# Output stores at slots of their own on a second queue, a spread issued behind the next copy, and one reciprocal per query denominator, with a retimed plan

## The chip, the core and the metric

The kernel runs on one core of one Trainium2 chip. The core has five engines that run at the same time, each with its own in-order instruction queue: TensorE (PE, matrix products into PSUM), VectorE (DVE), ScalarE (ACT), GpSimd (POOL), and SyncE (SP), which here only issues DMA transfers. A DMA can be issued from SP's queue or from ACT's; an instruction that waits holds everything behind it on its own queue. The metric is the device time of one execution in microseconds (us), smaller is better.

## The reference

```python
B, S, D, H = 1, 2048, 640, 32          # Dh = 20; F = 1536
xn = layernorm(x)
q, k, v = heads(xn @ wqkv)
pq, pk = q @ w_phi, k @ w_phi                          # per head, 20x20
phi_q = concat([softmax(pq), softmax(-pq)])            # 40 features per head
phi_k = concat([softmax(pk), softmax(-pk)])
kv = einsum("bhsf,bhsd->bhfd", phi_k, v)
z  = einsum("bhsf->bhf", phi_k)
num = einsum("bhqf,bhfd->bhqd", phi_q, kv)
den = einsum("bhqf,bhf->bhq", phi_q, z)[..., None] + 1e-6
s = merge_heads(num / den) @ wo                        # attention branch
g = silu(gelu(xn @ w1 + b1) @ w2 + b2)                 # gate branch
out = x + s * g
```

All arrays are 32-bit floats. Products that need full accuracy are made of three passes over high and low parts of both operands (high x high, high x low, low x high).

## The kernel before, in words

There are two halves. The first (to about 238 us) normalises x, makes keys, values and queries, and sums `kv` and `z`. It is not touched by the change. The second half runs PE through a **feed-forward** of 12 units and then a **tail**.

*A unit* takes two of the twelve 128-wide tiles of F for one half of the tokens (units 0 to 5 the first half, 6 to 11 the second). Its up projection (line 1275) is seven groups of products from sums of inputs and weights, with the sums undone on DVE (lines 1630 to 1652); ACT applies gelu (`act`) and makes the high part of the hidden layer, DVE the low part (`act_lo`, line 1286). Its down projection (`down`, line 1317) is ten groups of six matmuls, two times five output groups, each added into `y` by DVE (line 1326).

*Alongside*, DVE, ACT, POOL and SP do the rest of the attention for 16 token tiles `t`: load the exponentials (`q_load`), multiply by `z` on POOL (`q_ez`), sum per head (`q_rc`, `q_dn`), combine the sums into one factor per head and sign (`q_den`), scale (`q_scale`, on POOL or DVE), transpose (`q_turn`) and store the features (`q_put2`). They also load and split the weights of later units (`w2_load`, `w2_split`, `w1_step`), rebuild sums of x (`x_load` to `x_store`) and load them (`reload`).

*The tail* has four chunks `c` of 512 tokens. For each, `num_step` multiplies the features by `kv`: step 5 first (eight leftover heads), then 0 to 4. In each of these ACT copies the high part (line 1450) and DVE makes the low part (line 1451). `spread(j)` is a DMA from ACT's queue that puts the leftover rows into tile `j`. `finish(c, d)` then makes output group `d` (128 of the 640 columns): 15 matmuls (line 1514), times the gate on DVE (line 1516), plus x on POOL (line 1517), and a store. Gates of chunks 0 and 1 come from `y` through a silu on ACT (`gate`); those of chunks 2 and 3 were stored earlier and are loaded by `load_res` (line 1492), which also loads the x tile (line 1487).

*The order of the work* is written out by hand. PE's program has 372 + 40 slots: 31 in each unit, two in each output group of the tail. `tick()` emits what `PLAN` has put at the present slot, in order of the fraction; `when(s, f)` puts a call there. So a slot number says behind which other instructions an operation stands on its own engine's queue, and no more: an engine with nothing to wait for runs ahead. `PLAN["c_q"]`, `"c_w2"`, `"c_w1"` and `"c_x"` choose POOL or DVE for single operations. Tiles come from pools with a fixed number of buffers (`slabs` 23, `rows` 11, `phs` and `gts` for leftover features and gates in the tail); a new tile waits for the last user of its buffer. PSUM has eight banks, one for each product group.

In the tail a store of output group (c, d) is put two slots behind the group, on SP's queue:

```python
when(at_slot[0] + 2, nc.sync.dma_start, out_t[d * P:(d + 1) * P, c * CW:(c + 1) * CW], xr[:])
```

Because it is emitted through `tick`, the profile gives it line 1303. The stores of the last two groups are issued directly, in two halves each (line 1519).

Of the kernel before, what the change touches and what calls it, by code (L numbers as in the profile page):

```python
# [15 lines left out]
P = 128  # L16
# [24 lines left out]
def _ft(t):  # L41
# [2 lines left out]

PLAN = {
# [17 lines left out]
    ],  # L63
    "w2": [
        [-36.8, -32.04, 4.35, 3.86],
        [-0.55, 1.21, 31.1, 32.11],
        [28.2, 22.21, 57.6, 53.86],
        [64.2, 66.21, 95.6, 93.61],
        [93.95, 90.46, 124.6, 125.36],
        [120.45, 122.96, 154.85, 156.86],  # L70
        [156.45, 155.46, 183.85, 185.11],
        [192.95, 189.71, 219.6, 219.61],
        [219.95, 222.21, 249.1, 251.61],
        [250.7, 243.96, 278.1, 280.11],
        [279.95, 280.46, 312.85, 312.36],
        [302.2, 305.21, 343.1, 341.11],
    ],
    "w1": [
        [],
        [0.15, 7, 10.6, 15.5, 17, 17.5],  # L80
        [36.15, 43.75, 51.1, 46.75, 47.75, 48.25],
        [62.65, 73, 77.85, 76.5, 77.0, 77.0],
        [92.65, 101.5, 107.1, 107.5, 108.5, 110.0],
        [119.9, 131.75, 138.85, 132.25, 133.25, 134.75],
        [155.9, 165.75, 168.85, 170.75, 172.75, 172.75],
        [187.15, 196.5, 203.1, 203.75, 205.0, 205.75],
        [232.5],
        [264.5],
        [281.25],
        [308.4, 318.0, 323.6, 323.0, 324.0, 324.75],  # L90
    ],
    "keep": [63.0, 90.5, 127.25],
    "x": [
        [26.75, 45.5, 52.3, 66.25, 73.8],
        [63.25, 84.25, 92.8, 107.75, 114.3],
    ],
    "reload": [157.35, 164.11, 160.37, 161.63, 165.89, 162.9, 164.41, 171.17],
    "silu": [191.5, 187.5, 201.75, 195.6, 197.95],
    "wo": [344.15, 334.16, 342.92, 333.43, 336.69, 356.75, 358.5, 361.5, 360.75, 361.75],
    "phi": [  # L100
        [340.85, 341.11, 338.87, 338.13, 337.39, 337.9],
        [359.75, 358.26, 352.52, 355.53, 356.79, 357.05],
        [371.5, 375.75, 372.75, 375.0, 376.0, 377.25],
        [387.25, 387.5, 387.0, 387.75, 390.25, 387.25],
    ],
    "num": [362.01, 377.01, 382.01, 396.01],
    "res": [361.25, 363.1, 374, 373.25, 376, 378.5, 381.5, 380.5, 387.25, 385, 386.5, 388, 395.25, 392.5, 393, 397.75, 395.5, 402.75, 401.0, 406.75],
    "gate": [371.9, 370.91, 375.15, 376.4, 378.9, 378.9, 378.9, 382.4, 385.65, 386.9, 392.65, 392.9, 393.9, 398.9, 396.15, 402.4, 406.9, 403.4, 408.9, 403.9],
    "c_x": ["pool", "pool", "pool", "pool"],
    "c_q": ["pool", "pool", "pool", "pool", "pool", "vector", "pool", "pool", "pool", "pool", "pool", "pool", "pool", "pool", "pool", "vector"],  # L110
    "c_w2": ["pool", "pool", "pool", "pool", "pool", "pool", "vector", "pool", "pool", "pool", "pool", "pool", "pool", "vector", "vector", "pool", "vector", "vector", "vector", "pool", "pool", "pool", "pool", "pool"],
    "c_w1": ["vector", "pool", "pool", "pool", "pool", "vector", "pool", "pool", "vector", "pool", "pool", "pool", "pool", "vector", "pool", "pool", "vector", "pool", "vector", "pool", "pool", "pool", "pool", "pool", "pool", "pool", "pool", "pool", "pool", "pool", "pool", "vector", "pool", "pool", "pool", "pool", "vector", "pool", "pool", "vector", "vector", "vector", "pool", "pool", "vector", "pool", "pool", "pool"],
    "c_wo": ["pool", "pool", "pool", "pool", "pool"],
    "c_oT": ["late", "slab", "late", "slab"],
}

# [2 lines left out]
def hedgehog_gated_mlp_kernel(ctx: ExitStack, tc: tile.TileContext, x, xt_in, wqk, bd, wv, wo, w1, b1, w2, b2, out_t):  # L119
# [1257 lines left out]
        qe[t].append(zv)  # L1377

    def q_rc(t):
        rc = head_sums(qe[t][0], "rc")  # L1380
        nc.vector.reciprocal(rc[:], rc[:])
# [4 lines left out]

    def q_den(t):
        rc, dn = qe[t][2:]
        nc.vector.tensor_tensor(dn[:], dn[:], rc[:], op=OP.mult)
        d3 = dn[:].rearrange("p (h s) -> p h s", s=2)  # L1390
        den = small.tile([P, 32], F32, tag="den", name="den")
        nc.vector.scalar_tensor_tensor(den[:], d3[:, :, 0], DEN_EPS, d3[:, :, 1], op0=OP.add, op1=OP.add)
# [110 lines left out]
    def finish(c, d, oT, last):  # L1503
# [109 lines left out]
    for unit in range(units):  # L1613
# [128 lines left out]
```

## Time and profile before

| what | value |
|---|---|
| runs | 654.72, 652.51, 651.80 us; median 652.51 |
| profiled execution | 652.12 us, its span 650.4 us |
| busy share of the span | PE 98%, PE weight loads 85%, DVE 73%, POOL 59%, ACT 46% |
| granted PE clock over the span | 0.997 |
| DMA | 130.58 MB, mean 201 GB/s |
| feed-forward, up to PE's first numerators of the tail | 238.20 to 545.2 us |
| tail | 545.2 to 650.4 us |

A group row reads: line, engine, operation, output tile <- input tiles, shapes, count | total us, mean ns of one | idle time of the engine just before, and what ended it. A row of the time table begins with its start and its duration in us; in brackets stands how long the engine sat idle before it, and what released it. A row of waits reads: engine, line, what was waited for: us in all, times, the longest. A row of windows has the stretch, its length, the busy time of PE, PE weight loads, DVE, ACT and POOL, then granted clock, DMA share and GB/s.

### The profile page before, as it was taken

How to read it: one execution, taken by the hardware profiler on the slowest of the kernel's cores; microseconds unless marked ns; L12 is line 12 of the kernel's file. 1: busy time of each engine (PE TensorE's matmuls, PEld its weight loads, DVE VectorE, ACT ScalarE, POOL GpSimd, SP SyncE). 2: the span in 40 equal slices, each digit the busy share in tenths (PEclk: the TensorE clock that was granted, in tenths of full speed). 3: DMA queues.
4: the chain of work that ended last, by engine and by line, in shares of the span. 5: the costliest groups of instructions: out<-in, count | busy, mean ns of one | idle time of the engine just before them, and what ended most of it. 6: DMA issues, size and time to landing. Idle time of an engine off the chain costs nothing.

```text
span 650.4 us, 11475 instructions
## 1 busy us (share of the span) xinstructions
PE 639.2 (98%) x4360; PEld 554.0 (85%) x4360; DVE 477.0 (73%) x737; ACT 301.1 (46%) x486; POOL 383.8 (59%) x333
## 2 busy tenths in 40 slices
PE   8999999999999999999999999999999999999797
PEld 8999999999999998888888888888888885758486
DVE  5879987766795666796778668987899897853232
ACT  4556777654566768435243255651231434342110
POOL 3597887775784446979875666335073866332332
PEclk9999999999999999999999999999999999999999
DMA  8436921130932882819939496695646699766955
GB/s 319 191 119 207 283 72 66 42 103 2 310 112 109 304 296 80 282 50 318 341 99 314 175 404 261 193 308 136 241 115 257 197 245 248 217 170 187 303 179 175
DMA packets 119938, 130.58 MB, mean 201 GB/s; under 512 B 46892, under 2 KB 86316, under 8 KB 118988
## 3 DMA queue, kind: packets, MB, share of 16 engines
q1 hardware_dynamic: 119564, 129.21, 61.7%
q10 hardware_dynamic: 320, 0.66, 0.5%
q8 instruction: 34, 0.56, 0.3%
q14 instruction: 20, 0.16, 0.1%
HBM read 81.66 MB, written 46.20 MB: 197 GB/s over the span
## 4 chain that ended last, share of the span: by engine, by line
PE 91%; DMA 3%; POOL 2%; issue 1%; DVE 1%; SPq 1%; ACT 0%; POOLq 0%; DVEq 0%
PE pB L1317 25%; PE pB L1275 22%; PE pW L558 21%; PE pB L1514 9%; PE pA L417 4%; PE pW L1051 3%; PE pB L1446 2%; DMA gt<-g_dram 2%; PE pA L236 2%; PE kv L650 1%; DMA folds<-in_wqk_dram 1%; POOL tt L349 1%; POOL xd L368 0%; PE pA L403 0%; PE pB L1249 0%
## 5 line engine op out<-in xcount | busy, mean ns | idle before, releaser
L1317 PE MATMUL pB<-hs,w2s 128*128 128x512 f32 x720 | 166.3, 390 | 0.8 <-DVE hs L1286 0.8
L1317 PEld LDWEIGHTS pB<-hs,w2s 128*128 128x128 f32 x720 | 134.9, 188 | 30.0 <-DVE hs L1286 1.2
L1275 PE MATMUL pB<-xp,w1s 128*128 128x512 f32 x324 | 81.3, 389 | 0.0
L475 POOL TENSOR_TENSOR eq<-eq,rc 128x1280 f32<-128x1280 f32 x14 | 33.4, 2389 | 79.2 <-DVE rc L1395 69.3
L1275 PE MATMUL pB<-xd,w1s 128*128 128x512 f32 x324 | 79.3, 389 | 0.0
L1326 DVE TENSOR_TENSOR y<-pB,y 128x512 f32<-128x512 f32 x100 | 64.4, 674 | 9.9 <-PE pB L1317 9.9
L1275 PEld LDWEIGHTS pB<-xd,w1s 128*128 128x128 f32 x324 | 60.8, 188 | 12.6
L1275 PEld LDWEIGHTS pB<-xp,w1s 128*128 128x128 f32 x324 | 60.8, 188 | 12.6
L1514 PE MATMUL pB<-oT,wo 128*128 128x512 f32 (+1 forms) x315 | 70.0, 382 | 0.1
L1514 PEld LDWEIGHTS pB<-oT,wo 128*128 128x128 f32 x315 | 57.3, 189 | 14.9 <-issue 3.0
L1280 ACT ACTIVATE pB<-pB,b1t 128x512 f32<-128x512 f32 x48 | 31.8, 662 | 69.7 <-DVE pB L1640 28.8
L456 POOL TENSOR_TENSOR e<-e,mxs 128x1280 f32<-128x1280 f32 x13 | 30.7, 2372 | 41.0 <-DVE mxs L451 29.5
L462 ACT ACTIVATE e<-e 128x1280 f32<-128x1280 f32 x32 | 40.8, 1274 | 17.5 <-POOL e L456 7.9
L558 PE MATMUL pW<-wsum,xd 128*128 128x320 f32 x288 | 48.4, 310 | 0.0
L1376 POOL TENSOR_TENSOR ez<-eq,zrep 128x1280 f32<-128x1280 f32 x16 | 47.4, 2967 | 1.5 <-PE pB L1317 1.5
L1291 ACT ACTIVATE x<-pB 128x512 f32<-128x512 f32 x12 | 7.2, 599 | 78.8 <-PE pB L1275 78.8
L558 PEld LDWEIGHTS pW<-wsum,xd 128*128 128x128 f32 x288 | 43.6, 188 | 0.0
L475 POOL TENSOR_TENSOR e<-e,rc 128x1280 f32<-128x1280 f32 x15 | 36.1, 2409 | 5.8 <-DVE rc L912 4.5
L1517 POOL TENSOR_TENSOR xres<-y,xres 128x256 f32<-128x256 f32 x20 | 14.1, 737 | 38.0 <-issue 22.3
L1286 DVE TENSOR_TENSOR hs<-pB,hs 128x512 fp32r<-128x512 f32 x48 | 31.8, 683 | 3.8 <-ACT hs L1282 3.8
L211 POOL TENSOR_TENSOR w2s<-raw,w2s 128x640 fp32r<-128x640 f32 x18 | 28.7, 1609 | 10.0 <-ACT w2s L209 10.0
L674 POOL TENSOR_TENSOR w1s<-raw,w1s 128x384 fp32r<-128x384 f32 (+1 forms) x14 | 19.0, 1360 | 23.1 <-ACT w1s L673 23.1
(218 smaller groups left out, 1272.8 us busy)
## 6 DMA issues: line engine op xcount, KB each, us to landing
raw<-in_w_dram SPq DMA_DIRECT2D x42, 320.0 KB
e_dram<-e SPq DMA_DIRECT2D x16, 640.0 KB
eq<-e_dram SPq DMA_DIRECT2D x16, 640.0 KB
phi_dram<-pt SPq DMA_DIRECT2D x64, 160.0 KB
ph<-phi_dram SPq DMA_DIRECT2D x20, 480.0 KB
xt<-in_x_dram SPq DMA_DIRECT2D x16, 320.0 KB
xres<-in_xt_dram SPq DMA_DIRECT2D x20, 256.0 KB
out_dram<-xres SPq DMA_DIRECT2D x18, 256.0 KB
```

What stands on the lines that cost most here:

```text
L211: eng.tensor_tensor(sl[:, 1, :], raw, sl[:, 0, :].bitcast(F32), op=OP.subtract)
L456: eng.tensor_tensor(e3, e3, mx[:, :, None].to_broadcast([P, 64, DH]), op=OP.subtract)
L462: nc.scalar.activation(ef, ef, AF.Exp)
L475: eng.tensor_tensor(e3, e3, rc[:, :, None].to_broadcast([P, 64, DH]), op=OP.mult)
L558: nc.tensor.matmul(self.bank[ch][:, :HALF], self.x(blk, a), w(b), start=new and i == 0, stop=i == len(mms) - 1, skip_group_check=True)
L1275: nc.tensor.matmul(bank[ch][:], tl[:, a, off + wo_:off + wo_ + P], mov(blk, b), start=new and n == 0, stop=n == len(mms) - 1, skip_group_c ...
L1280: nc.scalar.activation(ps, ps, AF.Gelu_apprx_tanh, bias=b1t[:, f:f + 1])
L1286: nc.vector.tensor_tensor(hs[:, 1], ps, hs[:, 0].bitcast(F32), op=OP.subtract)
L1317: nc.tensor.matmul(ps[:], ws[i][:, b, d * P:(d + 1) * P], hs[o][i][:, a, :], start=i == n == 0, stop=(i, n) == (GF - 1, 2), skip_group_che ...
L1326: nc.vector.tensor_tensor(y, ps[:], y, op=OP.add)
L1376: nc.gpsimd.tensor_tensor(zv, qe[t][0], zf_at[0], op=OP.mult)
L1514: nc.tensor.matmul(ps[:, cols], w, o[:, a, cols], start=n == 0, stop=n == 14)
```

## The change

1. The whole-tile stores of the tail go to a queue named in `PLAN["c_st"]` (here ACT's for every one) at a number of slots behind their group that is named in `PLAN["st"]` (0 to 4.5).
2. `spread(j)` is issued behind the copy of step `j + 1`; the last one behind its own copy.
3. `q_rc` no longer takes the reciprocal of the per-head sums of the two signs. It writes the two sums crossed over, and `q_den` multiplies with them, so that one reciprocal of 32 columns is left. The value is the same up to rounding.
4. The tail has two `phs` buffers instead of three, and four `gts` buffers instead of three.
5. Nearly every number of `PLAN` moves, mostly by a few slots; some operations change between POOL and DVE.

```diff
 "q" (16 rows, here three):
-        [156.25, 171.0, 180.0, 183.0, 185.0, 185.1, 192.0, 193.0, 213.75, 209.1],
+        [151.75, 167.0, 176.0, 178.0, 180.0, 180.1, 187.0, 188.0, 208.75, 204.35],
-        [327, 337, 348.5, 352.6, 354, 354.1, 367.5, 369],
-        [368, 369.1, 372.8, 374, 375, 375.1, 377, 377.1, 377, 378.6],
+        [335, 345, 356.5, 360.6, 362, 362.1, 367.5, 369],
+        [367.75, 369.35, 373.05, 374.25, 375.25, 376.35, 377.25, 378.35, 378.25, 379.85],
...
     "x": [
-        [63.25, 84.25, 92.8, 107.75, 114.3],
+        [63.0, 81.0, 88.55, 103.75, 108.3],
...
-    "reload": [157.35, 164.11, 160.37, 161.63, 165.89, 162.9, 164.41, 171.17],
+    "reload": [156.35, 164.11, 166.12, 162.88, 165.89, 165.9, 166.41, 176.17],
...
     "phi": [
-        [387.25, 387.5, 387.0, 387.75, 390.25, 387.25],
+        [384.0, 384.25, 383.75, 386.5, 387.75, 387.75],
     ],
-    "num": [362.01, 377.01, 382.01, 396.01],
-    "res": [361.25, 363.1, 374, 373.25, 376, 378.5, 381.5, 380.5, 387.25, 385, 386.5, 388, 395.25, 392.5, 393, 397.75, 395.5, 402.75, 401.0, 406.75],
+    "num": [362.01, 378.26, 382.76, 394.26],
+    "res": [360.25, 363.1, 374.25, 367.75, 372.5, 377.25, 375.5, 379.5, 383.25, 381.25, 382.5, 384, 393.0, 388.5, 390, 394.25, 390.5, 398.25, 398.5, 399.25],
...
-    "c_x": ["pool", "pool", "pool", "pool"],
+    "c_x": ["pool", "vector", "pool", "vector"],
...
+    "st": [4, 3, 3, 0, 3, 3, 4.5, 4, 3, 3, 3, 3, 3, 0, 3, 3, 2, 3, 3, 3],
+    "c_st": ["scalar", ... 20 times],
@@ def q_rc(t):
-        rc = head_sums(qe[t][0], "rc")
-        nc.vector.reciprocal(rc[:], rc[:])
+        rc = small.tile([P, 64], F32, tag="rc", name="rc")
+        nc.vector.tensor_reduce(rc[:].rearrange("p (h s) -> p h s", s=2)[:, :, ::-1],
+                                qe[t][0].rearrange("p (h s d) -> p h s d", s=2, d=DH), axis=AX.X, op=OP.add)
@@ def q_den(t):
+        d3, r3 = (a[:].rearrange("p (h s) -> p h s", s=2) for a in (dn, rc))
+        nc.vector.scalar_tensor_tensor(d3[:, :, 0], r3[:, :, 1], DEN_EPS, d3[:, :, 0], op0=OP.mult, op1=OP.add)
         nc.vector.tensor_tensor(dn[:], dn[:], rc[:], op=OP.mult)
-        d3 = dn[:].rearrange("p (h s) -> p h s", s=2)
         den = small.tile([P, 32], F32, tag="den", name="den")
-        nc.vector.scalar_tensor_tensor(den[:], d3[:, :, 0], DEN_EPS, d3[:, :, 1], op0=OP.add, op1=OP.add)
+        nc.vector.tensor_tensor(den[:], d3[:, :, 0], d3[:, :, 1], op=OP.add)
         nc.vector.reciprocal(den[:], den[:])
-        r3 = rc[:].rearrange("p (h s) -> p h s", s=2)
         nc.vector.tensor_tensor(r3, r3, den[:, :, None].to_broadcast([P, 32, 2]), op=OP.mult)
@@ def num_step(c):
-        if j < 5:
+        if 0 < j < 5:
+            spread(j - 1, oTs[c])
+        if j == 4:
             spread(j, oTs[c])
@@ def finish(c, d, oT, last):
-            when(at_slot[0] + 2, nc.sync.dma_start, out_t[d * P:(d + 1) * P, c * CW:(c + 1) * CW], xr[:])
+            q = {"sync": nc.sync, "scalar": nc.scalar}[PLAN["c_st"][KC * ORDER.index(c) + d]]
+            when(at_slot[0] + PLAN["st"][KC * ORDER.index(c) + d], q.dma_start,
+                 out_t[d * P:(d + 1) * P, c * CW:(c + 1) * CW], xr[:])
@@ last unit
-            tailp.append(ctx.enter_context(tc.tile_pool(name="phs", bufs=3)))
-            tailp.append(ctx.enter_context(tc.tile_pool(name="gts", bufs=3)))
+            tailp.append(ctx.enter_context(tc.tile_pool(name="phs", bufs=2)))
+            tailp.append(ctx.enter_context(tc.tile_pool(name="gts", bufs=4)))
```

The numbers of a row of `"q"` are the slots of load, product with `z`, `q_rc`, `q_dn`, `q_den`, scale and the two transposes, and for odd tiles of the two stores; of `"x"` load, sum of parts, sums, split and store. `"phi"` has a chunk's six feature loads, `"num"` its numerators, `"res"` the 20 loads of x and gate tiles. In `"c_x"` the first two entries are the splits, the last two the sums of parts. `"c_q"` has four entries on DVE after the change and two before, `"c_w2"` three and six, and of the entries of `"c_w1"` that are used nine and seven.

More of the change, by code (lines that the diff above doesn't have):

```diff
@@ L46 @@
     "q": [
[16 rows of a table removed]
[16 rows of a table added]
     ],
     "w2": [
-        [-36.8, -32.04, 4.35, 3.86],
+        [-37.8, -32.04, 5.35, 6.86],
         [-0.55, 1.21, 31.1, 32.11],
[L67 to L76, printed above, removed]
+        [29.2, 22.71, 58.6, 52.86],
+        [64.2, 65.71, 95.1, 93.11],
+        [93.95, 94.46, 125.6, 125.36],
+        [125.45, 125.96, 157.85, 154.86],
+        [155.2, 154.96, 183.35, 185.61],
+        [192.95, 188.71, 218.6, 219.11],
+        [219.2, 222.46, 247.35, 249.86],
+        [250.45, 243.71, 278.85, 279.86],
+        [279.7, 280.46, 313.85, 312.36],
+        [302.2, 305.21, 345.1, 341.61],
     ],
@@ L79 @@
         [],
[L80 to L90, printed above, removed]
+        [-0.85, 7, 10.6, 15.5, 16, 17.5],
@@ L91 @@
+        [36.15, 43.75, 52.1, 47.75, 48.75, 49.25],
+        [61.65, 74, 78.85, 79.5, 78.5, 79.0],
+        [93.65, 102.5, 109.1, 108.5, 109.5, 111.0],
+        [118.9, 130.75, 137.85, 131.25, 132.25, 133.75],
+        [155.9, 165.75, 168.85, 170.75, 170.75, 171.75],
+        [185.65, 195.0, 201.6, 202.25, 203.5, 204.25],
+        [225.0],
+        [263.0],
+        [277.75],
+        [308.9, 318.5, 323.6, 322.0, 324.0, 324.75],
     ],
-    "keep": [63.0, 90.5, 127.25],
+    "keep": [62.0, 88.25, 127.75],
@@ L93 @@
     "x": [
-        [26.75, 45.5, 52.3, 66.25, 73.8],
-        [63.25, 84.25, 92.8, 107.75, 114.3],
-    ],
-    "reload": [157.35, 164.11, 160.37, 161.63, 165.89, 162.9, 164.41, 171.17],
-    "silu": [191.5, 187.5, 201.75, 195.6, 197.95],
-    "wo": [344.15, 334.16, 342.92, 333.43, 336.69, 356.75, 358.5, 361.5, 360.75, 361.75],
+        [23.75, 44.0, 53.05, 64.25, 71.8],
+        [63.0, 81.0, 88.55, 103.75, 108.3],
+    ],
+    "reload": [156.35, 164.11, 166.12, 162.88, 165.89, 165.9, 166.41, 176.17],
@@ L100 @@
+    "silu": [191.5, 186.75, 202.5, 197.85, 200.95],
+    "wo": [341.4, 330.91, 341.17, 334.18, 331.44, 357.75, 359.75, 364.5, 361.0, 360.75],
     "phi": [
-        [340.85, 341.11, 338.87, 338.13, 337.39, 337.9],
-        [359.75, 358.26, 352.52, 355.53, 356.79, 357.05],
-        [371.5, 375.75, 372.75, 375.0, 376.0, 377.25],
-        [387.25, 387.5, 387.0, 387.75, 390.25, 387.25],
-    ],
-    "num": [362.01, 377.01, 382.01, 396.01],
-    "res": [361.25, 363.1, 374, 373.25, 376, 378.5, 381.5, 380.5, 387.25, 385, 386.5, 388, 395.25, 392.5, 393, 397.75, 395.5, 402.75, 401.0, 406.75],
@@ L112 @@
-    "c_w1": ["vector", "pool", "pool", "pool", "pool", "vector", "pool", "pool", "vector", "pool", "pool", "pool", "pool", "vector", "pool", "pool", "vector", "pool", "vector", "pool", "pool", "pool", "pool", "pool", "pool", "pool", "pool", "pool", "pool", "pool", "pool", "vector", "pool", "pool", "pool", "pool", "vector", "pool", "pool", "vector", "vector", "vector", "pool", "pool", "vector", "pool", "pool", "pool"],
+        [337.1, 339.86, 335.62, 330.13, 331.39, 332.65],
+        [360.0, 360.01, 352.27, 357.28, 358.54, 359.55],
@@ new lines @@
+        [371.5, 375.75, 372.25, 374.5, 376.0, 377.0],
+        [384.0, 384.25, 383.75, 386.5, 387.75, 387.75],
+    ],
+    "num": [362.01, 378.26, 382.76, 394.26],
+    "res": [360.25, 363.1, 374.25, 367.75, 372.5, 377.25, 375.5, 379.5, 383.25, 381.25, 382.5, 384, 393.0, 388.5, 390, 394.25, 390.5, 398.25, 398.5, 399.25],
+    "gate": [371.9, 370.91, 375.15, 376.4, 379.15, 376.9, 378.4, 382.4, 385.65, 386.9, 392.65, 391.9, 393.9, 400.65, 396.15, 405.4, 406.9, 403.4, 408.9, 402.9],
+    "c_x": ["pool", "vector", "pool", "vector"],
@@ new lines @@
+    "c_q": ["pool", "pool", "pool", "pool", "pool", "vector", "vector", "pool", "pool", "pool", "pool", "pool", "pool", "pool", "vector", "vector"],
+    "c_w2": ["pool", "pool", "pool", "pool", "pool", "pool", "pool", "pool", "pool", "pool", "pool", "pool", "pool", "vector", "pool", "pool", "pool", "vector", "vector", "pool", "pool", "pool", "pool", "pool"],
+    "c_w1": ["vector", "pool", "pool", "pool", "pool", "vector", "pool", "pool", "vector", "pool", "pool", "pool", "pool", "vector", "pool", "vector", "vector", "pool", "vector", "vector", "pool", "pool", "pool", "pool", "pool", "pool", "pool", "pool", "vector", "pool", "pool", "vector", "pool", "vector", "pool", "vector", "vector", "pool", "vector", "vector", "vector", "vector", "pool", "pool", "pool", "pool", "pool", "pool"],
@@ L113 @@
     "c_wo": ["pool", "pool", "pool", "pool", "pool"],
+    "st": [4, 3, 3, 0, 3, 3, 4.5, 4, 3, 3, 3, 3, 3, 0, 3, 3, 2, 3, 3, 3],
+    "c_st": ["scalar", "scalar", "scalar", "scalar", "scalar", "scalar", "scalar", "scalar", "scalar", "scalar", "scalar", "scalar", "scalar", "scalar", "scalar", "scalar", "scalar", "scalar", "scalar", "scalar"],
     "c_oT": ["late", "slab", "late", "slab"],
@@ L1688, in hedgehog_gated_mlp_kernel @@
             finish(c, d, oTs[c], ci == NCH - 1 and d >= 3)
-    for _ in range(3):
+    for _ in range(12):
         tick()
```

3 lines of the change are left out of this document (removed), and 26 rows, old and new, of the table PLAN.

## The prediction

> **What bounds the kernel now.** I read the page's busy table first, then what TensorE (PE) waited for from 236 us on, then the chain of waits, and the time table of the one place where both pointed. The change touches nothing before 236 us.
>
> ```profile
> span 650.4 us, 11475 instructions
> PE 639.2 (98%) x4360; PEld 554.0 (85%) x4360; DVE 477.0 (73%) x737; ACT 301.1 (46%) x486; POOL 383.8 (59%) x333
> PE pB L1446 <- DVE oT L1451: 3.1, 1, 3.1
> PE pB L1317 <- DVE hs L1286: 0.8, 1, 0.8
> PE pB L1446 <- DMA ph<-phi_dram: 0.4, 1, 0.4
> 600.73 11.65 DMA gt<-g_dram
> ```
>
> PE is the bound, so only time in which PE stands or runs slowly can be won. Those three waits are all of them after 236 us: 3.10 + 0.81 + 0.42 (two decimals in the rows below). Two lie in the tail, where the chain leaves PE for an 11.65 us transfer of a gate tile.
>
> ```profile
> 612.48 0.76 DVE L1516 TENSOR_TENSOR gt<-pB,gt 128x256 f32<-128x256 f32 x2 [6.63 <-DMA gt<-g_dram]
> 608.38 0.63 PE L1454 MATMUL pB<-ph,bdl 80*40 80x256 f32 x4
> 609.43 2.80 PE L1446 MATMUL pB<-ph,bdk 120*64 120x512 f32 x12 [0.42 <-DMA ph<-phi_dram]
> 615.33 3.05 PE L1446 MATMUL pB<-ph,bdk 120*64 120x512 f32 x8 [3.10 <-DVE oT L1451]
> ```
>
> VectorE (DVE) sits 6.63 us in front of one gate product. The numerator copies of the last chunk stand behind it on DVE, so no PSUM bank comes free and PE stops 3.10 us. Why the transfer was late stands on SyncE's (SP's) queue:
>
> ```profile
> SPq L1303 <- POOL xres L1517: 12.0, 4, 5.4
> 580.47 2.12 SPq L1414 DMA_DIRECT2D phi_dram<-pt  x4
> 585.53 0.69 SPq L1487 DMA_DIRECT2D xres<-in_xt_dram  x1
> 594.61 0.33 SPq L1303 DMA_DIRECT2D out_dram<-xres  x1
> 596.02 0.39 SPq L1433 DMA_DIRECT2D ph<-phi_dram  x1
> 605.39 0.35 SPq L1433 DMA_DIRECT2D ph<-phi_dram  x1
> 592.00:594.00 2.00, 2.00 (x10) 1.66 (x9) 1.99 (x5) 0.68 (x2) 0.87 (x2) 1.00 0.14 20
> 602.00:604.00 2.00, 2.00 (x11) 1.65 (x10) 0.52 (x2) 0.00 (x0) 0.00 (x0) 1.00 1.04 249
> 616.00:618.00 2.00, 2.00 (x6) 0.30 (x2) 0.48 (x1) 0.60 (x1) 0.00 (x0) 0.51 1.06 358
> 618.00:620.00 2.00, 2.00 (x7) 1.43 (x6) 0.64 (x2) 0.60 (x1) 0.00 (x0) 0.64 0.83 295
> ```
>
> In the last four rows the two final columns but one are granted clock and DMA share. From 586.2 to 594.6 SP holds an output store that waits for GpSimd (POOL), with the last chunk's loads behind it; the transfer engines are at 0.14. When it goes, everything goes at once, the share is 1.04, and the gate tile queues behind the feature tiles. After the stall the granted clock is 0.51 and 0.64 for 2 us each: (1 - 0.51) x 2 + (1 - 0.64) x 2 = 1.70 us more.
>
> **Part 1, stores at slots of their own, on ScalarE's (ACT's) queue.** All 18 whole-tile stores leave SP, so SP no longer waits for POOL before it loads. The last chunk's feature loads move three slots earlier in the plan and the gate tiles get four buffers instead of three. SP's next hold-up ahead of those loads is the last feature store (580.47 to 582.59); behind it they can issue from about 583, 12 us sooner, into a stretch with free transfer engines. The last numerator step moves two slots forward, in front of one more output group of 15 matmuls (3.40 us at 226.7 ns, which is 13.60 us over 60 matmuls, quoted below). PE reaches it at 608.38 - 0.81 - 3.40 = 604.2. The chunk's six feature loads then have 21 us; before, they took from 596.02 to about 609. I put the gain at both tail waits and the clock: 3.10 + 0.42 + 1.70 = 5.22 us. The other end is that none of it comes, 0.
>
> What the stores cost ACT: an issue there takes 0.57 us in the rows below (SP's store rows 0.33), so 18 x 0.57 = 10.3 us on an engine that is busy 46% of the span. On PE's path that is nothing, if no store waits long. By plan slot, stores (1,1), (1,2) and (1,3) are ahead of the last numerator copies on ACT. The last of them needs POOL's add of chunk 1 group 3; PE ends that group two groups (6.8 us) before 604.2, and DVE 0.76 and POOL 2 x 0.737 us follow, so it is free 4 us before the copies.
>
> ```profile
> L1517 POOL TENSOR_TENSOR xres<-y,xres 128x256 f32<-128x256 f32 x20 | 14.1, 737 | 38.0 <-issue 22.3
> ```
>
> The new wait on SP: gate tile (3,1) is the fifth for four buffers and waits for POOL's add of (2,0), with the tiles (2,2), (3,0), (3,2), (3,3) and (3,4) behind it. (2,2) then needs the buffer of (2,1): with PE through that group at 604.2 + 5.0 (the last numerators: 0.63 for four matmuls, 2.80 for twelve, so 4.7 for twenty, which overlap a little) + 3.40 = 612.6, and 2.2 us more on DVE and POOL, it issues at 614.8 and lands between at once and 11.65 us later. PE ends (2,2) at 616.0, so DVE stands 0 to 10.5 us. No numerator copy is queued behind it then, and eight banks hold eight groups, 27 us: PE loses 0 at both ends.
>
> **Part 2, spread behind the next copy.**
>
> ```profile
> 583.44 0.60 ACT L1450 ACTIVATE oT<-pB 128x512 fp32r<-128x512 f32 x1
> 584.07 0.69 DVE L1451 TENSOR_TENSOR oT<-pB,oT 128x512 fp32r<-128x512 f32 x1 [0.20 <-ACT oT L1450]
> 584.79 0.58 ACTq L1463 DMA_DIRECT2D oT<-oTl  x1
> 585.42 0.60 ACT L1450 ACTIVATE oT<-pB 128x512 fp32r<-128x512 f32 x1 [1.38 <-DVE oT L1451]
> ```
>
> Today a step costs ACT 585.42 - 583.44 = 1.98 us, of which 0.75 is waiting for DVE's low part. With the next copy in between, it is 0.60 + 0.57 + 0.08 = 1.25; the five steps end about 3 us sooner in each chunk. I count 0: after a chunk's numerators PE has two to four groups, or half a down projection, to work on before it uses them, 6.8 us and more, and none of its three waits is for the output projection's operands.
>
> **Part 3, one reciprocal.**
>
> ```profile
> L1381 DVE RECIPROCAL rc<-rc 128x64 f32<-128x64 f32 x16 | 8.9, 553 | 0.5
> L1392 DVE SCALAR_TENSOR_TENSOR den<-dn 128x32 f32<-128x32 f32 x16 | 4.1, 254 | 0.5
> ```
>
> Each tile loses the 553 ns reciprocal and gains a 32-column product, which the trace does not show: above 0 and below the 553 ns of the 64-column operation; I take the 32-column row's 254. DVE gets 16 x 0.30 = 4.8 us back. DVE is not the bound, so by itself 0.
>
> **Part 4, the retimed plan.** The third PE wait:
>
> ```profile
> 535.28 0.69 DVE L1644 TENSOR_TENSOR pB<-u,pB 128x512 f32<-128x512 f32 x1 [0.95 <-PE pB L1275]
> 535.88 1.48 DVE L470 TENSOR_REDUCE rc<-eq 128x64 f32<-128x1280 f32 x1
> 538.54 6.64 PE L1317 MATMUL pB<-hs,w2s 128*128 128x512 f32 x28 [0.81 <-DVE hs L1286]
> ```
>
> The head sums of tile 14 (slot 348.5) come on DVE ahead of the hidden layer's low halves. The new plan has them at 356.5, and nothing of DVE's at slots 345 to 351: gain 0.81 us (bounds 0 and 0.81).
>
> It also takes work from POOL to DVE: one 1152-wide split and one 1280-wide sum, two more query scalings, two more splits of the first weights; three second-weight splits go the other way. The dangerous one is the 1152-wide split, now at slot 103.75, in DVE's order ahead of the first output copy and the low half that PE needs 6.8 us into the down projection:
>
> ```profile
> 330.17 13.60 PE pB L1317 x60
> 332.30 0.60 ACT L1282 ACTIVATE hs<-pB 128x512 fp32r<-128x512 f32 x1
> 332.93 0.69 DVE L1326 TENSOR_TENSOR y<-pB,y 128x512 f32<-128x512 f32 x1 [1.41 <-PE pB L1317]
> 333.54 0.68 DVE L1286 TENSOR_TENSOR hs<-pB,hs 128x512 fp32r<-128x512 f32 x1
> L1355 ACT ACTIVATE xhi<-xlo 128x1152 fp32r<-128x1152 f32 x2 | 2.3, 1156 | 0.0
> L475 DVE TENSOR_TENSOR eq<-eq,rc 128x1280 f32<-128x1280 f32 x2 | 3.0, 1492 | 0.1
> L674 DVE TENSOR_TENSOR w1s<-st,w1s 128x512 fp32r<-128x512 f32 x3 | 5.9, 1966 | 1.6 <-ACT w1s L673 1.6
> ```
>
> PE needs the low half at 330.17 + 6.80 + 0.45 = 337.4. ACT's copy for the split ends at 332.90 + 1.16 = 334.06; the split takes 1.34 us by the 1280-wide row (1492 x 1152/1280) or 4.4 by the 512-wide one (1966 x 1152/512); then 1.3 us for copy and low half: 336.7 or 339.8, a stall of 0 to 2.4. I take 0, since POOL has only short work there. The other retimings leave weights and reloads due at least as early against their use; I count 0.
>
> The page "SBUF — State Buffer" of the Trainium skill (section "SBUF: two separate sides") says that a DVE instruction with two SBUF inputs and a GpSimd one lock each other out of a shared port. The trace agrees that such a lock may be at work: 1966 ns for 512 columns beside 1492 for 1280. By that rule the sum would carry the 2.4 us.
>
> **Sum.** 5.22 + 0.81 = 6.03 us. The profiled execution took 652.12 us, 1.72 outside its span; its forecast is 646.1. It is 0.39 below the median of the runs shown, 652.51, from which the sum gives 646.5. I say 646.3.
>
> **Rivals.**
> *B, the transfers are the bound.* The stores and loads move the same bytes, the share from 596 to 616 was about 1, and the last gate or feature tile still lands late; only the 0.81 us comes: 652.12 - 0.81 = 651.3. For it: 1.04. Against: 0.14 just before. The Trainium skill's page "DMA: Bandwidth & Descriptors" (section "Issuing engines are not separate DMA queues") takes its side: a second issuing engine saves only issue time, for all run on the same 16 engines. The share of 0.14 at 592 says that what was short was not engines but an unblocked queue, which the rule does not speak of.
>
> *C, the retimed plan brings a stall of its own* in the 310 us of the feed-forward, first of all the 2.4 us above: 646.3 + 2.4 = 648.7.
>
> *D, slower: ACT inherits SP's wait.* The last numerator's copies stand on ACT behind stores.
>
> ```profile
> 614.62 0.69 DVE L1451 TENSOR_TENSOR oT<-pB,oT 128x512 fp32r<-128x512 f32 x1 [0.20 <-ACT oT L1450]
> 616.27 0.57 ACTq L1463 DMA_DIRECT2D oT<-oTl  x1
> SPq L1370 <- DMA ph<-phi_dram: 6.4, 1, 6.4
> ```
>
> The spread at 616.27 came 0.96 us after its data (615.31), and SP itself waited 6.4 us for an earlier transfer to land before another issue: an issue can be held by transfers in flight. If two of the three stores ahead of the copies each wait one long landing (2 x 11.65 = 23.3 us), PE fills the eight banks (six numerators, two groups: 604.2 to 616.0, less the 0.60 + 0.69 us of copies that return the first) and stands 23.3 - 10.5 = 12.8 us, plus 1.7 of clock: 646.3 + 14.5 = 660.8. It stalls PE from a delay of 10.5 us and makes the kernel slower than before from about 15. Against it: with the loads spread out, landings should be short.
>
> **Chances.** The forecast 57%, B 20%, C 13%, D 10%. What a measurement here can tell from no change is about 0.5%, 3.3 us: faster is below 649.2, slower above 655.8. Faster takes the forecast and most of C: 0.68. Same takes B and the rest of C and a short D: 0.23. Slower takes the rest of D: 0.09. The range holds the forecast, C and B. Its low end is 644.9: the lowest run shown is 0.71 under the median, and I allow that twice. Its high end is B plus the 0.4 by which the median stands over the profiled execution and as much again, 652.1. D and the tails are left out.
>
> **What would show it.** PE should have no wait for the numerator copies and a granted clock near 1.00 after 600 us; no SP store should wait for POOL, and the last chunk's feature loads should be out before 593; DMA share should be above 0.3 at 586 to 594 and below 1 at 600 to 612. ACT's copies should stand 1.25 to 1.3 us apart. The stall in front of the last unit's down projection should be gone, and the one at 337 absent (C if not). Wrong would be a PE wait of over 2 us in the tail, on gate tiles (B) or with ACT's store issue named as its releaser (D).

## The result, and the profile after

The changed kernel takes 647.11 us (median of 7 runs, 644.89 to 650.45), against 652.51 for the kernel before: ratio 0.9914, 95% interval 0.9885 to 0.9943. The prediction was 646.3 with a range from 644.9 to 652.1. The number came out; the experiments below show that the reason given for it was only a part of the reason.

The page of the changed kernel, and all that PE waited for from 236 us on (line, what was waited for: us in all, times, longest):

```profile
span 645.1 us, 11476 instructions
PE 637.5 (99%) x4360; PEld 554.0 (86%) x4360; DVE 473.7 (73%) x740; ACT 300.6 (47%) x486; POOL 374.7 (58%) x330
PE pB L1519 <- ACT y L1505: 1.4, 1, 1.4
PE pB L1519 <- DMA oT<-oTl: 0.3, 1, 0.3
```

The three waits of before (3.10, 0.81 and 0.42 us) are gone, and two new ones stand at the first output group of chunk 0. In the tail the rows that answer to those of before, first the time table, then the windows (last columns but one: granted clock, DMA share):

```profile
543.55 0.63 PE L1457 MATMUL pB<-ph,bdl 80*40 80x256 f32 x4
582.80 0.44 SPq L1436 DMA_DIRECT2D ph<-phi_dram  x1
590.57 4.96 SPq L1436 DMA_DIRECT2D ph<-phi_dram  x4
619.33 0.76 DVE L1521 TENSOR_TENSOR gt<-pB,gt 128x256 f32<-128x256 f32 x2 [4.70 <-DMA gt<-g_dram]
635.65 5.57 PE L1519 MATMUL pB<-oT,wo 128*128 128x512 f32 x38
```

```profile
592.00:594.00 2.00, 2.00 (x10) 1.65 (x9) 0.79 (x3) 0.00 (x0) 2.00 (x3) 1.00 0.91 237
602.00:604.00 2.00, 2.00 (x10) 1.68 (x9) 0.76 (x2) 0.00 (x0) 1.43 (x2) 1.00 1.04 331
616.00:618.00 2.00, 2.00 (x11) 1.65 (x10) 0.00 (x0) 0.00 (x0) 0.00 (x0) 1.00 0.48 130
```

The last chunk's feature loads go out from 582.80 (before, 596.02), the transfer engines are at 0.91 where they were at 0.14, the clock stays at 1.00, and a gate tile still makes DVE wait 4.70 us without PE losing anything. From its first numerators to its last matmul PE takes 543.55 to 641.22, 97.67 us; before, 545.12 (row below) to 646.51, 101.39. That is 3.72 us less: the 5.22 us of the forecast's tail came off and 1.73 us of new waits went on, which leaves 3.49. Of the other 1.6 us between the two spans, 0.43 came before PE's first product of the feed-forward, where nothing was changed (238.03 us before, 237.60 after), 0.81 is the old stall there, and for 0.33 no cause is shown.

### The profile page after: what moved, and what is told of

It reads as the page before. It is cut to its first block, busy times and chain, and to the rows that moved or that the text cites. A ratio compares the mean times of both kernels' runs of the same rounds, so it can differ in the third digit from the quotient of the medians.

```text
span 645.1 us, 11476 instructions
## 1 busy us (share of the span) xinstructions
PE 637.5 (99%) x4360; PEld 554.0 (86%) x4360; DVE 473.7 (73%) x740; ACT 300.6 (47%) x486; POOL 374.7 (58%) x330
## 4 chain that ended last, share of the span: by engine, by line
PE 93%; POOL 2%; DVE 2%; DMA 1%; issue 1%; ACT 1%; ACTq 0%; POOLq 0%
PE pB L1319 24%; PE pB L1277 23%; PE pW L560 21%; PE pB L1519 10%; PE pA L419 4%; PE pW L1053 3%; PE pB L1449 2%; PE pA L238 2%; PE kv L652 2%; PE pA L729 1%; POOL tt L351 1%; DMA oT<-oTl 1%; DMA xres<-in_xt_dram 1%; DVE y L1328 0%; POOL xd L370 0%
## 5 line engine op out<-in xcount | busy, mean ns | idle before, releaser
L477 POOL TENSOR_TENSOR eq<-eq,rc 128x1280 f32<-128x1280 f32 x12 | 28.7, 2392 | 60.5 <-DVE rc L1398 40.5
L213 POOL TENSOR_TENSOR w2s<-raw,w2s 128x640 fp32r<-128x640 f32 x21 | 33.4, 1601 | 12.2 <-ACT w2s L211 12.2
L1522 POOL TENSOR_TENSOR xres<-y,xres 128x256 f32<-128x256 f32 x20 | 15.5, 797 | 28.4 <-issue 13.9
L211 ACT ACTIVATE w2s<-raw 128x640 fp32r<-128x640 f32 x24 | 17.1, 734 | 28.0 <-PE pB L1319 21.9
```

The lines of the kernel that those rows point to most:

```text
L213: eng.tensor_tensor(sl[:, 1, :], raw, sl[:, 0, :].bitcast(F32), op=OP.subtract)
L477: eng.tensor_tensor(e3, e3, rc[:, :, None].to_broadcast([P, 64, DH]), op=OP.mult)
```

## The experiments

All twelve are timed against the kernel before on the same chip. Three chips were used, and the kernel before took 653.11 us (rows 2 to 5), 651.85 (rows 6 to 9) and 652.83 (the rest), so rows of different chips are compared by their ratios. "Old" and "new" stand for the kernel before and the changed one.

| stores on | spread order | plan and buffers | other | us | ratio, 95% interval |
|---|---|---|---|---|---|
| ACT | new | new | the changed kernel | 647.11 | 0.9914, 0.9885 to 0.9943 |
| SP | new | new | | 647.89 | 0.9928, 0.9903 to 0.9953 |
| SP | new | new | stores 8 slots late | 649.08 | 0.9950, 0.9926 to 0.9974 |
| ACT | old | old | | 656.60 | 1.0061, 1.0037 to 1.0085 |
| ACT | old | new | | 661.19 | 1.0129, 1.0095 to 1.0162 |
| SP | old | new | | 651.84 | 0.9994, 0.9977 to 1.0011 |
| SP | new | old | | 647.06 | 0.9910, 0.9890 to 0.9929 |
| ACT | new | old | | 646.50 | 0.9905, 0.9884 to 0.9925 |
| ACT | old, by POOL | new | | 647.41 | 0.9923, 0.9903 to 0.9943 |
| SP | new in chunk 2 | old | | 647.94 | 0.9931, 0.9910 to 0.9951 |
| SP | new in chunk 3 | old | | 652.24 | 0.9995, 0.9978 to 1.0013 |
| ACT | new | new | tile 14's denominators later | 645.71 | 0.9898, 0.9870 to 0.9926 |
| ACT | new | old | tile 14's sums later | 645.92 | 0.9889, 0.9864 to 0.9915 |

The first three columns were run in all eight combinations (old, old and SP is the kernel before). The four with the new spread order took 646.50 to 647.89 us, the four with the old one 651.84 to 661.19.

### Is it the queue of the stores?

The first theory was that of the prediction: SP must not wait for POOL at the head of its queue.

```diff
-    "c_st": ["scalar", ... 20 times],
+    "c_st": ["sync", ... 20 times],
```

> The changed kernel with its 18 whole-tile stores on SyncE's queue again, at the same slots and with everything else as changed. Theory (what was short in the tail was a queue that does not wait): SyncE waits for POOL's adds in front of loads again, the last chunk's loads go out late, and most of the 5.2 us of the tail comes back: about 651 us (649.5 to 652.5), with a PE wait of 2 to 3 us after 600 us and a granted clock well under 1 behind it. Rival (the retimed loads, the fourth gate buffer and the earlier last numerator step are enough by themselves): as the changed kernel, 646.5 to 647.8, with no PE wait after 600 us.

647.89 us: the rival's number, to 0.1 us. With the stores back on SP at the new slots, SP waits 1.4 us for POOL on stores, and PE has one wait, in chunk 0 as the changed kernel has:

```profile
PE pB L1519 <- ACT y L1505: 2.0, 1, 2.0
SPq L1305 <- POOL xres L1522: 1.4, 2, 0.8
```

So the queue is worth nothing that these runs can tell (0.9928 beside 0.9914). The rule of the Trainium skill that the prediction set beside rival B (page "DMA: Bandwidth & Descriptors", section "Issuing engines are not separate DMA queues") agrees with this pair.

```diff
-    "st": [4, 3, 3, 0, 3, 3, 4.5, 4, 3, 3, 3, 3, 3, 0, 3, 3, 2, 3, 3, 3],
+    "st": [8, 8, ... 20 times],
```

> The changed kernel with the 18 stores on SyncE's queue, but each 8 slots behind its group, where POOL's add should be long done. Theory (it is the wait at the queue's head and not the queue that the stores use): as the changed kernel, 646.5 to 648, with little or no SyncE time waiting for POOL on a store. Rival (SyncE simply has too much to issue, or an issue there is held by earlier landings): slower than the changed kernel by over 2 us, about 649 to 652, with loads late although no store waits for POOL.

649.08 us, at the low end of the rival's range, but by neither's mechanism. Nothing is late in the tail, where PE waits 0.2 us. But the stores that were put off pile up at the end:

```profile
635.81 3.98 PE L1519 MATMUL pB<-oT,wo 128*128 128x512 f32 x31
641.12 1.42 SPq L1305 DMA_DIRECT2D out_dram<-xres  x3
```

PE ends at 639.79, earlier than in the changed kernel, but three whole-tile stores are issued after that and the span ends at 646.3, 6.5 us behind PE instead of 3.9.

```diff
-            when(at_slot[0] + 2, nc.sync.dma_start, out_t[...], xr[:])
+            when(at_slot[0] + 2, nc.scalar.dma_start, out_t[...], xr[:])
```

> The kernel before, with one edit: its 18 whole-tile stores go to ScalarE's queue, at the old slots (two behind the group); plan, buffers, spreads and reciprocals stay as they were. Theory (the queue alone carries the tail's term of 5.2 us): SyncE no longer waits for POOL on a store, the feature loads go out before 593, the 3.10 us wait goes: 647 to 648.5. Rival (without the moved loads, the fourth gate buffer and the earlier numerator step the loads are still late, or ScalarE inherits the wait): 650.5 to 653, a PE wait of over 2 us after 600 us staying.

656.60 us: slower than before, outside both ranges, and the theory has fallen. The 3.10 us wait is gone from the list, but PE now waits 8.5 us, in four places, for spreads (the profiled execution is the slowest, 661.05):

```profile
PE pB L1514 <- DMA oT<-oTl: 8.5, 4, 5.8
```

The stores' queue takes the old stall away, but something else in the change is needed to keep this new one off.

### Is it the order of the spreads?

```diff
-        if 0 < j < 5:
-            spread(j - 1, oTs[c])
-        if j == 4:
+        if j < 5:
             spread(j, oTs[c])
```

> The changed kernel with each spread issued directly behind its own copy again. Theory (counted 0): ScalarE's copies stand 2.0 us apart again, chunk 0's last spread comes some 0.5 to 3 us later, and the time is that of the changed kernel to 0.5 us, 646.6 to 647.7; chunk 0's wait at its first output groups, 1.73 us in the changed kernel's trace, would grow by at most 1 us. Rival (the spread order is worth its own 3 us a chunk, since PE waits for the spread in chunk 0): 649 to 650, with the wait at chunk 0's first output groups at 4 to 5 us.

661.19 us: 14 us for an edit counted at nothing, and far above the rival as well. PE's waits, and then ACT's rows in chunk 2:

```profile
PE pB L1517 <- DMA oT<-oTl: 10.0, 5, 4.7
```

```profile
599.79 0.60 ACT L1453 ACTIVATE oT<-pB 128x512 fp32r<-128x512 f32 x1 [4.99 <-DMA xres<-in_xt_dram]
605.67 0.60 ACT L1453 ACTIVATE oT<-pB 128x512 fp32r<-128x512 f32 x1 [5.28 <-DMA gt<-g_dram]
612.09 0.60 ACT L1453 ACTIVATE oT<-pB 128x512 fp32r<-128x512 f32 x1 [5.83 <-DMA ph<-phi_dram]
```

The copies read nothing that these loads bring. Between two of them stands a spread, and the spread's issue is what waits. The built program shows for what: it deals eight completion semaphores out in turn over the transfers of SP and ACT together, so an issue waits until the transfer eight places earlier, on either queue, has landed. For chunk 2 these are:

| kernel | spread 0 | 1 | 2 | 3 | 4 |
|---|---|---|---|---|---|
| before | feature store | feature store | output store | x load | x load |
| before, new spread order | feature store | feature store | output store | x load | x load |
| changed | feature store | x load | gate load | feature load | spread 0 |
| changed, old spread order | feature store | x load | gate load | feature load | feature load |

In the last row the x load, gate load and feature load are the three releasers in ACT's rows above, in that order. They are later loads than those of the changed kernel: there the gate load is the chunk's first, here its second, and here the two feature loads are the last two of chunk 3 where there it is the first.

The next three runs separate this wait from the pitch of the copies (1.98 us old, 1.25 new, as the prediction worked out). The first has two of the edits shown so far, the stores on SP at the new slots and the old spread order.

> The changed kernel with stores on SyncE's queue and the old spread order: what is left of the change is the retimed plan, the store slots, the buffers and the single reciprocal. Theory (new after the first four runs: the built program deals eight completion semaphores out in turn over SyncE's and ScalarE's transfers together, and an issue waits until the transfer eight places earlier has landed, so a spread is held by a load of the other queue): here the middle chunk's spreads stand eight places behind a feature store, a residual load, the last chunk's first two feature loads and a residual load, which are older than the loads that held them in the run with ScalarE's stores and the old order (661.2 us), younger than those in the run with SyncE's stores and the new order (647.9). So between the two: 649 to 655 us, with ScalarE's copies in the middle chunk held by those loads. Rival (the pitch of ScalarE's copies, 2.0 us against 1.25, is what costs the 14 us): as the run at 661.2, 659 to 662. Second rival (spread order does not matter with stores on SyncE): 647 to 648.5.

651.84 us, in the theory's range. PE's waits, and ACT's rows in chunk 2:

```profile
PE pB L1517 <- DMA oT<-oTl: 3.7, 2, 2.6
PE pB L1449 <- DMA ph<-phi_dram: 1.3, 1, 1.3
```

```profile
596.75 0.60 ACT L1453 ACTIVATE oT<-pB 128x512 fp32r<-128x512 f32 x1 [6.23 <-DMA xres<-in_xt_dram]
601.35 0.60 ACT L1453 ACTIVATE oT<-pB 128x512 fp32r<-128x512 f32 x1 [4.00 <-DMA ph<-phi_dram]
```

Two copies are held, by an x load and a feature load. The 3.10 and 0.81 us waits of the kernel before are gone, and 5.0 us of others have come (of the 3.7 for spreads, 2.6 in chunk 0 and 1.1 in chunk 2). Stores at new slots, the retimed plan, the buffers and the single reciprocal **together gain nothing** while the spread order is old. The second run is the kernel before with the new order alone, the third has ACT's queue for the stores besides.

```diff
+        if 0 < j < 5:
+            spread(j - 1, oTs[c])
-        if j < 5:
+        if j == 4:
             spread(j, oTs[c])
```

> The kernel before with one edit: each spread issued behind the next step's copy. Theory (eight semaphores in turn): the middle chunk's spreads stand eight places behind two feature stores, an output store and two residual loads, all but one of them the same as before, and the stall of 3.10 us in the last chunk hangs on loads behind SyncE's wait for POOL, which this does not touch: as before, 652.0 to 653.6. Rival (the spread order by itself carries the gain): 647 to 649.5.

647.06 us: the rival. **This one edit to the kernel before gives all that the whole change gives**, and the semaphores do not explain it, for its spreads stand behind the same kinds of transfers as before, and in the kernel before all four waits of ACT between chunk 2's copies are the 1.37 or 1.38 us for DVE's low part that the prediction shows, and none is for a landing. Of the three old waits only the one in the feed-forward is left:

```profile
PE pB L1317 <- DVE hs L1286: 0.8, 1, 0.8
```

> The kernel before with its stores on ScalarE's queue and the new spread order, plan and buffers as before. Theory (eight semaphores in turn): in the middle chunk the spreads now stand eight places behind an output store, a residual load, two feature loads and a spread, instead of a residual load, a gate load, two residual loads and a spread in the run with ScalarE's stores and the old order (656.6): some 4 places older, so most of that run's 8.5 us of waits for spreads goes: 648 to 653 us. Rival (ScalarE's queue is itself the handicap with the old plan): 655.5 to 657.5.

646.50 us, better than the theory's range: with the new order the stores may be on either queue.

### How the pitch of the copies reaches the gate tile

PE's first numerators of the tail and of chunk 2, and DVE's rows, in the kernel before (SP's store at 594.61 stands in the prediction); then rows of DVE and SP in the same stretch with the new spread order alone:

```profile
545.12 0.63 PE L1454 MATMUL pB<-ph,bdl 80*40 80x256 f32 x4
579.50 0.63 PE L1454 MATMUL pB<-ph,bdl 80*40 80x256 f32 x4
580.36 2.04 DVE L1516 TENSOR_TENSOR y<-pB,y 128x256 f32<-128x256 f32 x6
591.98 0.69 DVE L1451 TENSOR_TENSOR oT<-pB,oT 128x512 fp32r<-128x512 f32 x1 [1.28 <-ACT oT L1450]
592.58 1.41 DVE L1516 TENSOR_TENSOR y<-pB,y 128x256 f32<-128x256 f32 x4
```

```profile
585.52 0.69 DVE L1451 TENSOR_TENSOR oT<-pB,oT 128x512 fp32r<-128x512 f32 x1 [0.53 <-ACT oT L1450]
587.59 0.76 DVE L1518 TENSOR_TENSOR y<-pB,y 128x256 f32<-128x256 f32 x2 [1.38 <-PE pB L1516]
589.61 0.33 SPq L1303 DMA_DIRECT2D out_dram<-xres  x1
595.54 0.34 SPq L1494 DMA_DIRECT2D gt<-g_dram  x1
```

In the kernel before, DVE's low parts keep ACT's pitch, and the gate products of the chunk before stand behind them on DVE: six halves (three groups) at 580.36 and four (two groups) at 592.58, back to back and waiting for nothing but their turn. POOL's adds, the store and the last chunk's loads follow. With the new order the last low part starts at 585.52 instead of 591.98, DVE waits for PE instead of PE's results for DVE, the store goes at 589.61 instead of 594.61, and the gate tile's load at 595.54 instead of 600.73. 6.5 us at the head of the chain are 5.2 at its end, enough to take PE's stall away. Of the 6.5, 2.5 had come by chunk 2's first low part (581.57 instead of 584.07, where it stood behind the six halves), and 4.0 come in its own steps.

Two runs test this against the thought that the gain is made in the last chunk, where PE's wait was: the new order in one chunk alone, first as in the diff, then with `c == 3`.

```diff
+        new = c == 2
+        if new and 0 < j < 5:
+            spread(j - 1, oTs[c])
-        if j < 5:
+        if j == 4 or (not new and j < 5):
             spread(j, oTs[c])
```

> The kernel before with the new spread order in chunk 2 alone (the third of four); chunks 0, 1 and 3 issue each spread directly behind its own copy. Theory (formed on the run with the new spread order alone, 647.06 us: ScalarE's pitch of 2.0 us sets the pitch of VectorE's low parts, the gate products of the chunk before stand behind these on VectorE, the residual adds and the store behind the products, and the last chunk's loads behind that store on SyncE): with 0.75 us less in each of five steps, and the backlog of products that chunk 1 still leaves, the store that SyncE waits for goes some 3 to 4 us earlier than before (594.61 us), the last gate tile lands as much earlier, and most of the 3.10 us wait, with its dip of the clock, goes: 647.5 to 650. Rival (the gain is made in the last chunk, whose own copies PE waited for): as before, 651.5 to 653.

> The kernel before with the new spread order in chunk 3 alone (the last). Theory (the gain is made upstream, in chunks 1 and 2): the last gate tile is as late as before, VectorE sits in front of its product, PE waits 3 us for the numerator copies: as before, 651 to 653. Rival (the gain is made in the last chunk): 647 to 648.5.

647.94 and 652.24 us, both as the theory has it: chunk 2 alone carries nearly the whole gain, chunk 3 alone none. The profiled execution of the first is its slowest (653.52): PE waits 3.1 us for spreads in chunk 0, which has the old order there. The long wait of the last chunk is not in it. Only distances within it are used:

```profile
585.66 0.63 PE L1454 MATMUL pB<-ph,bdl 80*40 80x256 f32 x4
596.27 0.33 SPq L1303 DMA_DIRECT2D out_dram<-xres  x1
```

From chunk 2's numerators on PE to the store that SP waits for it is 10.61 us, as with the new order in all chunks (579.00 to 589.61); before, 579.50 to 594.61, 15.11. In the second run the store goes at 595.23, the gate tile is as late as before, and PE stands at the same place, this time with a feature load as the last to come:

```profile
612.59 0.76 DVE L1519 TENSOR_TENSOR gt<-pB,gt 128x256 f32<-128x256 f32 x2 [6.38 <-DMA gt<-g_dram]
616.48 3.68 PE L1446 MATMUL pB<-ph,bdk 120*64 120x512 f32 x8 [3.86 <-DMA ph<-phi_dram]
```

That is the chain in the kernel before, and not the only way out of its stall. In the changed kernel two copies of chunk 2 are held by landings, and what follows is nearly as late as before:

```profile
585.68 0.60 ACT L1453 ACTIVATE oT<-pB 128x512 fp32r<-128x512 f32 x1 [2.86 <-DMA phi_dram<-pt]
588.35 0.34 SPq L1497 DMA_DIRECT2D gt<-g_dram  x1
590.14 0.60 ACT L1453 ACTIVATE oT<-pB 128x512 fp32r<-128x512 f32 x1 [3.16 <-DMA gt<-g_dram]
591.38 1.41 DVE L1521 TENSOR_TENSOR y<-pB,y 128x256 f32<-128x256 f32 x4
594.43 0.40 ACTq L1305 DMA_DIRECT2D out_dram<-xres  x1
```

Two groups' products go back to back at 591.38 (before, 592.58) and the store behind them at 594.43 (594.61). But that store stands on ACT's queue, and SP has sent the gate tile's load at 588.35 instead of 600.73. So here it is the freed queue that takes the stall away, as the prediction had it; the run at 646.50 shows the same (products at 591.74, store at 594.32). The old wait for the copies is also gone in the runs at 656.60, 661.19 and 651.84. **What sets these three apart is what came in its place**, PE's waits of 8.5, 10.0 and 3.7 us for spreads; with the new order in all chunks, PE's waits in the tail come to 2.0 us at most, all in chunk 0.

### The wait for landings by itself

```diff
-        nc.scalar.dma_start(oT[0][j][15::16].bitcast(F32), ...)
+        nc.gpsimd.dma_start(oT[0][j][15::16].bitcast(F32), ...)
```

> The run with ScalarE's stores and the old spread order (661.2 us), with its 20 spreads issued by GpSimd in place of ScalarE; their place in the program's text stays. In the built program they then take completion semaphores of their own, and none is eight places behind a load. Theory (it was that semaphore wait that held ScalarE's copies): ScalarE's copies in the middle chunk are no longer held by landings, PE's 10 us of waits for spreads go, 646 to 650 us. Rival (the spreads were late because the transfer engines are full at 594 to 614): the spreads land as late as before, PE still waits for them, 656 to 661.

647.41 us instead of 661.19, with the old place of the spreads in the text. Of PE's waits for spreads one of 1.3 us is left, in chunk 0. ACT's copies in chunk 2 now stand 0.86 us apart:

```profile
583.53 0.60 ACT L1453 ACTIVATE oT<-pB 128x512 fp32r<-128x512 f32 x1 [0.26 <-PE pB L1449]
584.39 0.60 ACT L1453 ACTIVATE oT<-pB 128x512 fp32r<-128x512 f32 x1 [0.26 <-PE pB L1449]
```

```profile
602.00:604.00 2.00, 2.00 (x10) 1.68 (x9) 0.76 (x2) 0.00 (x0) 1.02 (x2) 1.00 1.04 399
```

The transfer engines are as full (share 1.04 in this window), and PE is busy for all of its 2 us: full engines alone are not what made the spreads late. This edit takes away the wait for landings and the 0.75 us for DVE's low part at once; that the 14 us are mostly the first rests on the 5 to 6 us between the copies in the run at 661.19, which a pitch of 1.98 cannot make.

### The changed kernel's new wait, and the old one of 0.81 us

In the changed kernel, time table at the start of the tail:

```profile
544.23 0.38 ACT L1462 ACTIVATE oTl<-pB 40x256 fp32r<-40x256 f32 x1 [2.23 <-PE pB L1457]
547.87 0.38 ACT L1462 ACTIVATE oTl<-pB 40x256 fp32r<-40x256 f32 x1 [3.27 <-DVE oTl L1463]
549.63 1.16 ACTq L1466 DMA_DIRECT2D oT<-oTl  x1
557.15 0.93 PE L1519 MATMUL pB<-oT,wo 128*128 128x512 f32 x3 [0.29 <-DMA oT<-oTl]
559.53 8.44 PE L1519 MATMUL pB<-oT,wo 128*128 128x512 f32 x36 [1.44 <-ACT y L1505]
```

ACT waits 3.27 us for a low half that DVE makes only behind tile 14's denominators, which the new plan has at 360.6 to 362.1, just ahead of the numerators (362.01).

```diff
-        [335, 345, 356.5, 360.6, 362, 362.1, 367.5, 369],
+        [335, 345, 356.5, 363.0, 363.2, 363.3, 367.5, 369],
```

> The changed kernel with one edit of the plan: query tile 14's denominators (slots 360.6, 362 and 362.1) go to 363.0, 363.2 and 363.3, behind the first chunk's numerators. Theory (the changed kernel's new wait of 0.29 and 1.44 us at the first output group comes from VectorE, which has those denominators ahead of the low half of the first numerator step, so that the spreads go out late and land behind the next loads): chunk 0's spreads go out 1.5 to 3 us earlier, both waits go, 645.0 to 646.2. Rival (the transfer engines, full at 552 to 558, set the landing): as the changed kernel, 646.6 to 647.8, with the wait of 1.4 us staying.

645.71 us, and PE has no wait left from 236 us to the end:

```profile
544.10 0.63 PE L1457 MATMUL pB<-ph,bdl 80*40 80x256 f32 x4
545.64 0.38 ACT L1462 ACTIVATE oTl<-pB 40x256 fp32r<-40x256 f32 x1 [0.48 <-DVE oTl L1463]
547.39 1.16 ACTq L1466 DMA_DIRECT2D oT<-oTl  x1
555.89 6.28 PE L1519 MATMUL pB<-oT,wo 128*128 128x512 f32 x27
```

From PE's first numerators (544.10; 543.55 in the changed kernel) to the first spread it is 3.29 us instead of 6.08. The releaser named on the 1.44 us row, a silu on ACT, has nothing to do with PE's operands; which of the two, the spread's landing or the last split of the output weights (which ACT's copies push back too), ended that wait is not told apart.

```diff
 (on the kernel before, stores on ACT's queue and new spread order)
-        [327, 337, 348.5, 352.6, 354, 354.1, 367.5, 369],
+        [327, 337, 352.5, 352.6, 354, 354.1, 367.5, 369],
```

> The kernel before with stores on ScalarE's queue, the new spread order, and query tile 14's head sums moved from slot 348.5 to 352.5, behind the hidden layer's low halves. The first two gave 646.5 us with one wait of 0.8 us left, PE on a low half. Theory: the sums were ahead of that half on VectorE, the wait goes and nothing takes its place: 645.3 to 646.0. Rival (the later denominators push the next low half or the first numerator copies): 646.3 to 647.5, with a new wait of PE between 538 and 560.

645.92 us; the 0.8 us wait that its base still had is gone, and 0.2 us for a spread in chunk 0 has come, where the theory had nothing. This and the run at 645.71 have the two best medians. Both are ahead of the kernel before; by their intervals neither can be told from the changed kernel.

## Why the number was right and the reason only in part

**What bounds the kernel: right.** PE's three waits were the whole price, and the tail's stall came from a gate tile that was late because SP stood in front of a store that waited for POOL. Moving the stores, the new plan and the new spread order each take it away; it stays where only the last chunk has the new order.

**Part 1: its mechanism came, but it is neither enough nor needed.** In the changed kernel the waits behind the 5.22 us are gone, because SP runs ahead of a store that is as late as before. Its loads were out by 595.5 and not before 593, as SP waited 2.8 us for a feature load and 2.5 for an x load to land. But moving the stores by itself loses (656.60; with the new plan 661.19), and with the stores on SP the new spread order gives as much (647.06), by getting the late add itself out earlier. The prediction took that add as given.

**Part 2: the step that failed.** "I count 0" rested on who waits for a spread in the kernel before. It measured 4.8 us by itself (647.06 against 651.85 on the same chip) and 14 us within the change (661.19), where PE waits 10.0 us for spreads without it. The 0.75 us per step was worked out rightly. What was not asked is what else stands behind the low parts on DVE, and which landing a spread's own issue waits for once other transfers move. The prediction names for every added wait what is queued behind it, and did not do the same for the wait that goes. That the number held all the same is luck: the part counted at nothing was in the change.

**Part 3: 0, and nothing speaks against it.** It was not run alone. In the changed kernel the new operation, the 32-column sum that has replaced the one with the constant, and (for Part 4) the 1152-wide split are

```profile
L1393 DVE SCALAR_TENSOR_TENSOR dn<-rc,dn 128x32 f32<-128x32 f32 x16 | 7.1, 441 | 0.1
L1396 DVE TENSOR_TENSOR den<-dn 128x32 f32<-128x32 f32 x16 | 3.1, 192 | 0.6
333.50 1.36 DVE L1358 TENSOR_TENSOR xlo<-xlo,xhi 128x1152 fp32r<-128x1152 f32 x1 [2.41 <-ACT xhi L1357]
```

The new operation takes 441 ns where 254 was taken, but the other small ones are shorter than before (225, 192 and 225 ns instead of 337, 254 and 269), so a tile's five operations take 1.44 us instead of 1.77: 5.3 us in all against the 4.8 forecast. Two reciprocals per tile stand in the runs at 646.50 and 645.92, which are as fast.

**Part 4: 0.81 right, and a term missed.** The head sums were the cause: the wait stays in all five runs with the old plan and its sums, and goes in the last one. The 1152-wide split on DVE (last row above) took 1.36 us against 1.34, and PE did not wait behind it. But the row that moved the sums also moved the denominators in front of the first chunk's numerators: 1.73 us of waits that stood nowhere in the sum and go when the denominators are put back behind them (645.71).

**Signs that did not come.** The share was to be below 1 at 600 to 612 and is 1.04 at 602 to 604; ACT's copies were to stand 1.25 to 1.3 us apart and are held for 2.86 and 3.16 in chunk 2.

**Rival B** (transfers are the bound) falls with the share of 1.04 and no stall. **Rival C** (the plan brings a stall of its own) was true, though in chunk 0 and not at the 1152-wide split, and at 1.73 us instead of 2.4. **Rival D** (ACT inherits the wait) was a real danger. With the old spread order ACT stood still for landings and the kernel was slower than before, 656.60 and 661.19. It was not the stores ahead of the last copies that waited, as D had it, but the spreads among chunk 2's; that the second number is near D's 660.8 is chance. The argument given against it, short landings, is not what kept it off, for landings still hold two copies in the changed kernel: the new spread order is.

## What to carry to other kernels

When a wait is shortened, list what is queued behind it on its own engine and follow that list to the end of the chain, just as for a wait that is added; "nobody on the critical path reads this result" is not enough. A part that takes a wait away may bring another: in three runs here the old stall was gone and the kernel no faster. Before moving transfers between queues, look up which earlier transfer each issue waits for: queues that share completion semaphores are not independent. Undo the parts of a change one at a time even where the total is as forecast.

## What the runs showed that was not expected

- **A transfer's issue can hold an engine for 5 to 6 us on account of a transfer of another queue** (4.99, 5.28 and 5.83 us on ACT, each ended by a load that SP had issued). It is a property of the built program, eight semaphores dealt out in turn, not of the transfer engines.
- **Moving 18 stores of 256 KB from one queue to the other** changed the time by less than can be told with the new spread order (647.89 and 647.11; 647.06 and 646.50) and made it 0.6% and 1.4% slower with the old one (ratio 1.0061 against the kernel before, 1.0129 beside 0.9994).
- **A store issued late costs at the end**: three whole-tile stores behind PE's last product lengthened the end from 3.9 to 6.5 us.
